# A planner that counts VectorE's maxima, reciprocals, joins and low parts of x as ready later

## Chip, core and metric

The kernel runs on one core of one Trainium2 chip. The time is device microseconds (us) from the start to the end of one execution; a kernel's figure is the median of its runs. The engines are named as in the profile: PE (TensorE, matrix products; PEld its weight loads), DVE (VectorE), ACT (ScalarE), POOL (GpSimd) and SP (SyncE, which here issues every DMA).

## What is computed

Three stages follow each other, the first per head, the other two per token:

```python
scores = q @ k.T / sqrt(D)              # 4 batches, 8 heads, 576 x 576, D = 64
kth    = the 32nd largest of each row
attn   = softmax(where(scores >= kth, scores, -1e9))
x      = attn @ v                       # 2304 tokens x 512
h      = maximum(x @ w_in, 0)           # 512 -> 2048
x      = (h * h) @ w_out                # 2048 -> 512
h      = maximum(maximum(x @ w1, x @ w2), x @ w3)   # 512 -> 768
out    = h @ w_out2                     # 768 -> 512
```

The weights come as 64-bit floats. The kernel turns each half chunk of them (128 x 1024 numbers) into a pair of 32-bit parts, high and low, and multiplies with three products (high x high, high x low, low x high). The activations x and h are split into high and low parts in the same way.

## The kernel before

The 2304 tokens are dealt into six groups of 384 columns (group 0 to group 5). For each group the attention of its rows comes first, two heads at a time (four such pairs make the 512 columns of x), then the two feed-forward stages (`moe(g)`). A piece of attention is one head by 128 rows, a *job*: PE makes scores (L525), ACT scales them into `s` (L446), DVE finds the 32 largest by four MAX (L452) with three MATCH_REPLACE between (L454), ACT makes the exponentials `e` (L312, L460, L463), POOL their low halves, SP transposes them by DMA into `et` (L468), PE multiplies with v (L479). Behind some jobs stands the end of a tile: POOL adds a guard (L530), DVE takes the reciprocal `rc` (L532), POOL multiplies (L538), PE transposes (L505), ACT writes the high part of x into `xt` (L507), DVE the low part (L509; L491 and L493 for the remainder rows).

The weights of group 0 are converted on the way, 36 half chunks during the attention of group 0 (`cw`) and 20 more during `moe(0)` (`wt`): SP loads one (L588), ACT makes two pieces of it (`ot` L312 and `lw` L592), DVE joins them by bits (L594, the *join*), ACT rounds to the high part (L597), POOL subtracts for the low part (L309), SP stores the pair in DRAM (L599). Groups 1 to 5 read the pairs back (L576).

In `moe(g)` PE makes h (L630, stage 1), ACT squares (L654 to L656), POOL makes the low part `hl`, PE makes the second product into four banks `a` (stage 2); the result is split by ACT (L667) and DVE (L668, recorded at the helper's line L309). Of the three products of the second layer ACT copies the first into `m` (L680), DVE takes the maximum with the second and the third (L682, the *maxima*), ACT and POOL split the result. The last product (the output stage) reads the weights w_out2 and goes out by ACT (L712) and SP.

No order is written by hand. Every operation is first entered in a plan, with its engine, a priority and an estimated length, and `Plan.run` plays the five engines forward on those estimates: of an engine's operations it issues the one that could begin first, a little biased by priority, and that order then stands in the program for good. An operation is ready when the last of those that it reads has ended, plus a hop between engines, plus its `slack`:

```python
        def ready_at(o):
            t = 0.0
            for d in o.deps:
                t = max(t, d.end + hop(d.eng, o.eng))
            t += o.slack
```

So slack makes no engine wait on the chip. It only makes the plan believe that the operation comes later, so that others of its engine (and, through what reads its result, of other engines) are put ahead of it. `SL` is 1000 ns. Each engine executes its own list strictly in the planned order.

Of the kernel before, what the change touches and what calls it, by code (L numbers as in the profile page):

```python
# [10 lines left out]
F32 = mybir.dt.float32  # L11
# [255 lines left out]
def kernel(ctx, tc, q, k, v, w_in, w_out, w1, w2, w3, w_out2, out):  # L267
# [34 lines left out]
    def pe(prio, ns, reads, writes, fn):  # L302
        plan.op(PE, ns, prio, reads, writes, fn)

    def dma(prio, nbytes, reads, writes, fn, ns=650.0):
        plan.op(SP, ns, prio, reads, writes, fn, lat=max(nbytes / DBW, 90.0))

    def sub(eng, out_ap, a, b):
        eng.tensor_tensor(out_ap, a, b, op=ALU.subtract)  # L309
# [108 lines left out]
    def attend(i, unit, p):  # L418
        b, tl, rem, g, col = unit
        plan.bias = -10 if i == 0 else 0  # L420
        new = (b, p) not in kv
        if new:
            kt = prep_k(b, p)
        qt = prep_q(i, unit, p)
        plan.bias = 0
        if new:
            kv[b, p] = [kt, *prep_v(load_v(b, p))]
        kt, vt, us = kv[b, p]
        if (g, p) not in xt:
            t = buf("xt", [P, 2, KD, NW], F32R)  # L430
            xt.update({(g, d): (Slot(t, 0, d), Slot(t, 1, d)) for d in range(KD)})
        xh, xl = xt[g, p]
        xg = buf("xg", [P, XW, P]) if tl else None
        xs = None
        nt = len(tl)
        jobs = [(j, h) for j in range(nt) for h in range(2)] + ([(-1, 0)] if rem else [])
        for j, h in jobs:
            for _ in range(min(PER if g == 0 else 0, len(ahead))):
                half_chunk(False, *ahead.pop(0))
            s = buf("s", [P, S])  # L440
            for f in range(2):
                ps = buf("b", [P, 512])
                cs = slice(f * HS, (f + 1) * HS)
                pe(A_S, (4 * HS / 2.4 if b in PLAIN else 2 * c_mm(HS)) * (1 if j >= 0 else 2), [kt, qt], [ps, (s, f)],
                   scores(j, h, nt, qt, kt, ps, cs, b in PLAIN))
                act(A_S, HS, [ps], [(s, f)], lambda s=s, cs=cs, ps=ps: nc.scalar.activation(  # L446
                    s[:, cs], ps[:, 0:HS], AF.Copy, scale=escale))
            w_, mx, nb, e = buf("w", [P, S]), buf("mx", [P, 32]), buf("nb", [P, 1]), buf("e", [P, S])
            for r in range(4):
                src = s if r == 0 else w_  # L450
                m8 = slice(8 * r, 8 * r + 8)
                dve(A_X, S, [src], [(mx, r)], lambda src=src, mx=mx, m8=m8: nc.vector.max(out=mx[:, m8], in_=src[:]))  # L452
                if r < 3:
                    dve(A_X, S + 50, [src, (mx, r)], [w_], lambda src=src, mx=mx, m8=m8, w_=w_: nc.vector.match_replace(  # L454
                        out=w_[:], in_to_replace=mx[:, m8], in_values=src[:], imm_value=-3.0e38))
            gps(A_E, 110, [(mx, 0), (mx, 3)], [nb], lambda mx=mx, nb=nb: nc.gpsimd.tensor_scalar(  # L456
                nb[:], mx[:, 31:32], mx[:, 0:1], ebias, op0=ALU.subtract, op1=ALU.add))
            act(A_E, S, [s, (mx, 3)], [e], lambda s=s, e=e, mx=mx: prelu(
                e[:], s[:], KEEP, bias=mx[:, 31:32], scale=-1.0), psum=False, ptr=1)
            act(A_E, S, [e, nb], [e], lambda nb=nb, e=e: nc.scalar.activation(  # L460
                e[:], e[:], AF.Exp, bias=nb[:], scale=-1.0 / KEEP), psum=False, ptr=1)
            e16, et = buf("e16", [P, 2 * S], F16), buf("et", [P, 10, P], F16)
            act(A_E, S, [e], [(e16, 0)], lambda e=e, e16=e16: nc.scalar.copy(e16[:, S:2 * S], e[:]), psum=False)  # L463
            gps(A_E, 512, [e, (e16, 0)], [(e16, 2)], lambda e=e, e16=e16: sub(
                nc.gpsimd, e16[:, 0:512], e[:, D:S], e16[:, S + D:2 * S]))
            gps(A_E, D, [e, (e16, 0)], [(e16, 3)], lambda e=e, e16=e16: sub(
                nc.gpsimd, e16[:, 512:S], e[:, 0:D], e16[:, S:S + D]))
            dma(A_S, DTR * DBW, [e16], [et], lambda e16=e16, et=et: nc.sync.dma_start_transpose(et[:, 0:9], e16[:]), ns=1360.0)  # L468
            if j < 0 or (h == 0 and j % 2 == 0):
                xs = buf("xs", [P, 2, 2, VW])  # L470
            for hh, c0, c1 in ([(0, 0, D), (1, D, P)] if j < 0 else [(h, 0, P)]):
                ps = buf("b", [P, 512])
                m = c1 - c0

                def av(ps=ps, m=m, et=et, c0=c0, c1=c1, hh=hh):
                    for x, mm_ in enumerate(AVORD):
                        wv = VW2 if mm_ < 4 else VW
                        vc = mm_ if mm_ <= 4 else mm_ - 5
                        nc.tensor.matmul(ps[0:m, 0:wv], et[:, mm_, c0:c1], vt[:, hh, vc, 0:wv],  # L479
                                         start=x == 0, stop=x == 8)  # L480
                pe(A_E, 400.0, [et, vt], [ps, (xs, (max(j, 0) % 2, hh)), *([(xg, (j, hh))] if xg else [])], av)
                act(A_X, VW, [ps], [(xs, (max(j, 0) % 2, hh))], lambda ps=ps, xs=xs, m=m, j=j, hh=hh: nc.scalar.copy(  # L482
                    xs[0:m, max(j, 0) % 2, hh, :], ps[0:m, 0:VW]))
            if j < 0:
                xr = buf("xr", [P, P])
                finish_x(xs, D, 1, xr, lambda xr=xr: xr[0:D, :].unsqueeze(1))
                ps = buf("b", [P, 512])
                pe(A_X, 107.0, [xr], [ps, (xh, "r"), (xl, "r")], lambda xr=xr, ps=ps: nc.tensor.transpose(
                    ps[:, 0:D], xr[0:D, :], ident_t[0:D, 0:D]))
                cs = slice(rcol[b], rcol[b] + D)  # L490
                act(A_X, D, [ps, us], [(xh, "r")], lambda ps=ps, cs=cs: nc.scalar.activation(  # L491
                    xh[:, cs], ps[:, 0:D], AF.Copy, scale=us[:]), ptr=1)
                dve(A_S, D, [ps, us, (xh, "r")], [(xl, "r")], lambda ps=ps, cs=cs: nc.vector.scalar_tensor_tensor(  # L493
                    xl[:, cs], ps[:, 0:D], us[:], xh[:, cs].bitcast(F32), op0=ALU.mult, op1=ALU.subtract), slack=SL / 2)
            elif h == 1 and (j % 2 == 1 or j == nt - 1):
                j0 = j - j % 2
                finish_x(xs, P, j + 1 - j0, xg, lambda j0=j0, j=j: xg[:, j0:j + 1, :])
        if not tl:
            return
        w = nt * P  # L500
        ps = buf("b", [P, 512])

        def f():
            for c in range(nt):
                nc.tensor.transpose(ps[:, c * P:(c + 1) * P], xg[:, c, :], ident)  # L505
        pe(A_S, 107.0 * nt, [xg], [ps, (xh, col), (xl, col)], f)
        act(A_S, w, [ps, us], [(xh, col)], lambda: nc.scalar.activation(  # L507
            xh[:, col:col + w], ps[:, 0:w], AF.Copy, scale=us[:]), ptr=1)
        dve(A_S, w, [ps, us, (xh, col)], [(xl, col)], lambda: nc.vector.scalar_tensor_tensor(  # L509
            xl[:, col:col + w], ps[:, 0:w], us[:], xh[:, col:col + w].bitcast(F32),  # L510
            op0=ALU.mult, op1=ALU.subtract), slack=SL / 2)

    def scores(j, h, nt, qt, kt, ps, cs, plain):
        def run():
# [13 lines left out]
    def finish_x(xs, pn, nt, dst, xo):  # L528
        rc = buf("rc", [P, 2, 2, 1])
        gps(A_S, 100, [xs], [rc], lambda: nc.gpsimd.tensor_scalar(  # L530
            rc[0:pn, 0:nt], xs[0:pn, 0:nt, :, 0:1], eguard, 2.0, op0=ALU.add, op1=ALU.mult))
        dve(A_S, 4, [rc], [rc], lambda: nc.vector.reciprocal(rc[0:pn, 0:nt], rc[0:pn, 0:nt]))  # L532

        def part(x):
            return xs[0:pn, 0:nt, :, 1 + x * D:1 + (x + 1) * D]
# [33 lines left out]
    def half_chunk(again, n, x):  # L569
# [15 lines left out]
        def word(u):  # L585
# [7 lines left out]
            lw[:], bits(U8).rearrange("p (n u) -> p n u", u=8)[:, :, 3], AF.Copy, scale=1.0 / 32.0, bias=-15.5 / 32.0), psum=False)  # L593
        joined.append(dve(C_D, 512, [cv, lw], [cv], lambda: nc.vector.scalar_tensor_tensor(  # L594
            cv[:].bitcast(U32), cv[:].bitcast(U32), 3, lw[:], op0=ALU.logical_shift_left, op1=ALU.bitwise_or),
            rate=1.7, slack=SL / 2))
        act(C_A, 512, [cv], [(wt, 0)], lambda: nc.scalar.copy(wt[:, 0], cv[:]), psum=False)  # L597
        gps(C_P, 512, [cv, (wt, 0)], [(wt, 1)], lambda: sub(nc.gpsimd, wt[:, 1], cv[:], wt[:, 0].bitcast(F32)))
        dma(W_, P * 4096, [wt], [dst], lambda: nc.sync.dma_start(  # L599
            dst[:], wt[:].rearrange("p a b -> p (a b)").bitcast(F32)))  # L600
        return wt

    def moe(g):
# [61 lines left out]
        for d in range(KD):  # L665
            xh, xl = xs[d]
            act(MA, N, [acc[d]], [(xh, kx) for kx in xcols], lambda d=d, xh=xh: nc.scalar.copy(xh[:, 0:N], acc[d][:, 0:N]))  # L667
            dve(A_S, N, [acc[d], (xh, xcols[0])], [(xl, kx) for kx in xcols], lambda d=d, xh=xh, xl=xl: sub(  # L668
                nc.vector, xl[:, 0:N], acc[d][:, 0:N], xh[:, 0:N].bitcast(F32)), slack=SL / 4)
        h2 = []  # L670
        for fp in range(NF2):
            m = [buf("m0", [P, NW]), buf("m1", [P, NW])]
            for jj in range(3):
                w_, vw = nextw()
                for f in range(2):
# [4 lines left out]
                        act(MA, N, [ps], [m[f]], lambda ps=ps, m=m[f]: nc.scalar.copy(m[:, 0:N], ps[:, 0:N]))  # L680
                    else:
                        dve(A_S, N, [ps, m[f]], [m[f]], lambda ps=ps, m=m[f]: nc.vector.tensor_tensor(  # L682
                            m[:, 0:N], ps[:, 0:N], m[:, 0:N], op=ALU.max), slack=SL / 4)
                    if jj == 2:
                        hh, hl = buf("hh", [P, NW], F32R), buf("hl", [P, NW], F32R)
                        act(MA, N, [m[f]], [hh], lambda m=m[f], hh=hh: nc.scalar.copy(hh[:, 0:N], m[:, 0:N]), psum=False)
# [104 lines left out]
```

## Time and profile before

| | us |
|---|---|
| median of 3 runs (1076.82 to 1080.04) | 1076.9 |
| the profiled execution, its own time | 1079.8 |
| its span, first to last instruction | 1078.0 |
| PE busy in the span | 984.3 |
| DVE busy | 818.7 |
| ACT busy | 767.8 |
| POOL busy | 625.3 |

The span falls into stretches with different limits. Up to 200 us the attention of group 0 runs and weights are converted; PE is busy 122 us of it. From there PE is nearly always busy, with the feed-forward of one group and the attention of later groups mixed. The groups follow each other on PE: group 1 begins at 361.8 us, group 2 at 514.6, group 3 at 670.9, group 4 at 829.4, group 5 at 955.9. From about 890 us no attention is left, and PE works on groups 4 and 5 alone.

### The profile page before, as it was taken

What the parts mean: (1) busy time and instruction counts of PE and PEld (TensorE: products, weight loads), DVE (VectorE), ACT (ScalarE), POOL (GpSimd) and SP (SyncE); (2) the same over time, 40 slices, a digit from 0 to 9 for tenths busy, and PEclk for the clock granted to TensorE, in tenths of its full rate; (3) what the DMA queues carried; (4) which work ended last, traced back from release to release, by engine and by line L of the source; (5) the groups of instructions that cost most, each with busy time, mean ns of one, the idle gap of its engine ahead of it and who ended that gap; (6) DMA issues with size and microseconds to landing.
All of it is one profiled execution on the core that took longest, in us unless ns stands there. A gap on an engine that the chain in (4) does not pass through costs nothing.

```text
span 1078.0 us, 18812 instructions
## 1 busy us (share of the span) xinstructions
PE 984.3 (91%) x6116; PEld 889.7 (83%) x6116; DVE 818.7 (76%) x1736; ACT 767.8 (71%) x1616; POOL 625.3 (58%) x887
## 2 busy tenths in 40 slices
PE   5556576999998999999999999999999999999998
PEld 3333343799897899998999998999998999989997
DVE  5999899899976999999999999999999601100020
ACT  6987788899887889976788868888876742123311
POOL 2666677787787577756467676767565641112210
PEclk9999755799999999999999999999999999999999
DMA  9999899999998999999999999999999986787774
GB/s 306 348 308 251 256 285 332 245 269 231 251 341 318 316 348 283 288 288 256 300 261 266 281 284 274 267 237 262 254 256 280 285 261 237 252 266 262 257 239 147
DMA packets 249697, 295.04 MB, mean 274 GB/s; under 512 B 178944, under 2 KB 182528, under 8 KB 249600
## 3 DMA queue, kind: packets, MB, share of 16 engines
q1 hardware_dynamic: 249600, 293.85, 95.1%
q8 instruction: 48, 0.79, 0.3%
q14 instruction: 49, 0.40, 0.1%
HBM read 217.25 MB, written 34.08 MB: 233 GB/s over the span
## 4 chain that ended last, share of the span: by engine, by line
PE 61%; DVE 13%; ACT 11%; POOL 7%; DMA 4%; issue 3%; SPq 0%; POOLq 0%; ACTq 0%; DVEq 0%
PE a L630 37%; PE b L630 13%; DVE mx L452 7%; DVE w L454 6%; PE b L525 5%; PE b L479 4%; DMA xt<-in_moe_w_in_dram 2%; POOL e L309 2%; ACT s L446 1%; ACT e L312 1%; POOL hl L309 1%; DMA xt<-in_moe_w_dram 1%; ACT lw L592 1%; ACT e L460 1%; ACT ot L312 1%
## 5 line engine op out<-in xcount | busy, mean ns | idle before, releaser
L452 DVE MAX8 mx<-w 128x8 f32<-128x576 f32 x432 | 311.1, 746 | 0.1
L309 POOL TENSOR_TENSOR e<-e,e 128x512 f16<-128x512 f32 (+1 forms) x288 | 211.9, 748 | 108.6 <-ACT e L463 91.3
L630 PE MATMUL a<-xt,wt 128*128 128x384 f32 x1296 | 239.3, 339 | 1.0 <-DVE xt L309 0.9
L630 PE MATMUL b<-xt,wt 128*128 128x384 f32 x1152 | 235.9, 346 | 3.5 <-DMA wt<-wsc 1.9
L630 PE MATMUL a<-hh,wt 128*128 128x384 f32 x768 | 228.8, 346 | 0.0
L630 PEld LDWEIGHTS a<-xt,wt 128*128 128x128 f32 x1296 | 224.1, 188 | 2.2 <-DVE xt L309 1.9
L454 DVE MATCH_REPLACE8 w<-mx,w 128x576 f32<-128x576 f32 x288 | 213.1, 742 | 0.0
L630 PEld LDWEIGHTS b<-xt,wt 128*128 128x128 f32 x1152 | 203.8, 192 | 5.8 <-DMA wt<-wsc 1.9
L525 PE MATMUL b<-kt,qt 128*128 128x288 f32 (+1 forms) x640 | 167.9, 395 | 36.2 <-DMA qt<-in_q_dram 17.8
L309 POOL TENSOR_TENSOR hl<-r,hh 128x384 fp32r<-128x384 f32 x96 | 97.3, 1014 | 126.5 <-ACT hh L656 119.2
L525 PEld LDWEIGHTS b<-kt,qt 128*128 128x128 f32 (+1 forms) x640 | 118.1, 218 | 62.5 <-ACT xs L482 16.4
L630 PEld LDWEIGHTS a<-hh,wt 128*128 128x128 f32 x768 | 142.7, 190 | 2.1 <-issue 1.1
L630 PE MATMUL a<-hl,wt 128*128 128x384 f32 x384 | 131.3, 342 | 4.1 <-POOL hl L309 3.8
L312 ACT ACTIVATE e<-s,mx 128x576 f32<-128x576 f32 x144 | 112.2, 779 | 27.7 <-POOL e L309 16.5
L479 PEld LDWEIGHTS <-et 128*128 128x128 f16 (+1 forms) x1440 | 84.1, 108 | 57.6 <-issue 35.4
L446 ACT ACTIVATE s<-b 128x288 f32<-128x288 f32 x288 | 108.0, 409 | 24.8 <-PE b L525 23.2
L479 PE MATMUL b<-vt,et 128*128 128x129 f16 (+3 forms) x1440 | 101.7, 223 | 25.2 <-DMA et<-e 16.8
L460 ACT ACTIVATE e<-e,nb 128x576 f32<-128x576 f32 x144 | 112.1, 779 | 6.8 <-POOL nb L456 4.8
L452 DVE MAX8 mx<-s 128x8 f32<-128x576 f32 x144 | 107.2, 746 | 10.3 <-ACT s L446 10.3
L454 DVE MATCH_REPLACE8 w<-mx,s 128x576 f32<-128x576 f32 x144 | 106.8, 742 | 0.0
L654 ACT ACTIVATE r<-b 128x384 f32<-128x384 f32 x96 | 47.1, 490 | 79.2 <-PE b L630 76.6
L463 ACT CAST e<-e 128x576 f16<-128x576 f32 x144 | 96.6, 672 | 1.6 <-DMA et<-e 1.3
(62 smaller groups left out, 1194.8 us busy)
## 6 DMA issues: line engine op xcount, KB each, us to landing
wt<-wsc SPq DMA_DIRECT2D x316, 512.0 KB, 4.8
wsc<-cw SPq DMA_DIRECT2D x36, 512.0 KB, 4.9
xt<-in_moe_w_out_dram SPq DMA_DIRECT2D x22, 512.0 KB, 6.3
wsc<-wt SPq DMA_DIRECT2D x20, 512.0 KB, 5.7
xt<-in_moe_w_dram SPq DMA_DIRECT2D x18, 512.0 KB, 5.9
xt<-in_moe_w_in_dram SPq DMA_DIRECT2D x16, 512.0 KB, 5.8
ks<-in_k_dram SPq DMA_DIRECT2D x12, 576.0 KB, 5.9
vst<-in_v_dram SPq DMA_DIRECT2D x16, 320.0 KB, 5.8
```

What stands on the lines that cost most here:

```text
L309: eng.tensor_tensor(out_ap, a, b, op=ALU.subtract)
L312: return nc.scalar.activation(out_ap, src, AF.Prelu, alpha=slope, **kw)
L446: act(A_S, HS, [ps], [(s, f)], lambda s=s, cs=cs, ps=ps: nc.scalar.activation(s[:, cs], ps[:, 0:HS], AF.Copy, scale=escale))
L452: dve(A_X, S, [src], [(mx, r)], lambda src=src, mx=mx, m8=m8: nc.vector.max(out=mx[:, m8], in_=src[:]))
L454: dve(A_X, S + 50, [src, (mx, r)], [w_], lambda src=src, mx=mx, m8=m8, w_=w_: nc.vector.match_replace(out=w_[:], in_to_replace=mx[:, m8], ...
L460: act(A_E, S, [e, nb], [e], lambda nb=nb, e=e: nc.scalar.activation(e[:], e[:], AF.Exp, bias=nb[:], scale=-1.0 / KEEP), psum=False, ptr=1)
L463: act(A_E, S, [e], [(e16, 0)], lambda e=e, e16=e16: nc.scalar.copy(e16[:, S:2 * S], e[:]), psum=False)
L479: nc.tensor.matmul(ps[0:m, 0:wv], et[:, mm_, c0:c1], vt[:, hh, vc, 0:wv], start=x == 0, stop=x == 8)
L525: nc.tensor.matmul(ps[:, 0:HS], a, c, start=m == 0, stop=m == len(seq) - 1)
L592: act(C_M, 512, [raw], [lw], lambda: nc.scalar.activation(lw[:], bits(U8).rearrange("p (n u) -> p n u", u=8)[:, :, 3], AF.Copy, scale=1.0 ...
L630: nc.tensor.matmul(o, x, y, start=first and i == 0 and m == 0, stop=last and i == n - 1 and m == 2)
L654: act(MA, N, [ps], [r], lambda r=r, ps=ps: nc.scalar.activation(r[:, 0:N], ps[:, 0:N], AF.Relu))
```

## The change

The slacks of five kinds of DVE operations grow: the low parts of x in the attention (L509, L493) from 500 to 1500 ns, the reciprocals (L532) from 0 to 1000, the joins (L594) from 500 to 1000, the low parts between the two feed-forward stages (L668) from 250 to 750, the maxima (L682) from 250 to 2000. DMA issues get a slack too, which is zero. No instruction is added, removed or altered; the order on all five engines is planned anew.

```diff
-            dma(A_S, DTR * DBW, [e16], [et], lambda ...: nc.sync.dma_start_transpose(et[:, 0:9], e16[:]), ns=1360.0)
+            dma(A_S, DTR * DBW, [e16], [et], lambda ...: nc.sync.dma_start_transpose(et[:, 0:9], e16[:]), ns=1360.0, slack=0.0 * SL)
...
-                    xl[:, cs], ps[:, 0:D], us[:], xh[:, cs].bitcast(F32), op0=ALU.mult, op1=ALU.subtract), slack=SL / 2)
+                    xl[:, cs], ps[:, 0:D], us[:], xh[:, cs].bitcast(F32), op0=ALU.mult, op1=ALU.subtract), slack=1.5 * SL)
...
-            op0=ALU.mult, op1=ALU.subtract), slack=SL / 2)
+            op0=ALU.mult, op1=ALU.subtract), slack=1.5 * SL)
...
-        dve(A_S, 4, [rc], [rc], lambda: nc.vector.reciprocal(rc[0:pn, 0:nt], rc[0:pn, 0:nt]))
+        dve(A_S, 4, [rc], [rc], lambda: nc.vector.reciprocal(rc[0:pn, 0:nt], rc[0:pn, 0:nt]), slack=1.0 * SL)
...
-            rate=1.7, slack=SL / 2))
+            rate=1.7, slack=1.0 * SL))
...
-                nc.vector, xl[:, 0:N], acc[d][:, 0:N], xh[:, 0:N].bitcast(F32)), slack=SL / 4)
+                nc.vector, xl[:, 0:N], acc[d][:, 0:N], xh[:, 0:N].bitcast(F32)), slack=0.75 * SL)
...
-                            m[:, 0:N], ps[:, 0:N], m[:, 0:N], op=ALU.max), slack=SL / 4)
+                            m[:, 0:N], ps[:, 0:N], m[:, 0:N], op=ALU.max), slack=2.0 * SL)
```

On DVE, near the end of group 0's attention, from the reciprocal of the fourth pair of heads (`rc3`) to its low part (`xt1`), the kernel before has:

```order
L532 RECIPROCAL rc3_1717<-rc3_1717 128x2
L454 MATCH_REPLACE w1_1672<-mx3_1656,w1_1672 128x576
L452 MAX mx2_1638<-w0_1648 128x8
L452 MAX mx3_1656<-w1_1672 128x8
L452 MAX mx4_1751<-s4_1552 128x8
L594 SCALAR_TENSOR_TENSOR ot2_1741<-ot2_1741,lw1_1674 128x512
L454 MATCH_REPLACE w1_1672<-mx3_1656,w1_1672 128x576
L509 SCALAR_TENSOR_TENSOR xt1_773<-b3_1746,us3_544,xt1_773 128x384
```

and the changed kernel, at the same place:

```order
L532 RECIPROCAL rc3_1723<-rc3_1723 128x2
L594 SCALAR_TENSOR_TENSOR ot2_1728<-ot2_1728,lw1_1657 128x512
L454 MATCH_REPLACE w1_1685<-mx3_1663,w1_1685 128x576
L452 MAX mx4_1765<-s4_1525 128x8
L452 MAX mx3_1663<-w1_1685 128x8
L454 MATCH_REPLACE w0_1777<-mx4_1765,s4_1525 128x576
L452 MAX mx5_1783<-s5_1582 128x8
L509 SCALAR_TENSOR_TENSOR xt1_759<-b2_1760,us3_591,xt1_759 128x384
```

The reciprocal and the low part have moved three places down DVE's list (247 to 250 and 254 to 257): ahead of this low part stand two MAX and one MATCH_REPLACE more than before, and the same number of joins, reciprocals and other low parts.

On PE, at the passage from group 0's second layer (weights `wt0`, `wt6`) to its output stage (w_out2 in `wt1`, `wt2`, `wt3`), the kernel before has:

```order
L630 MATMUL a1_3917<-xt1_773,wt0_3828 128x384 x6
L630 MATMUL a2_3946<-wt1_3907,hh4_3554 128x512 x2
L630 MATMUL a2_3946<-wt1_3907,hl4_3591 128x512
L630 MATMUL a3_3952<-wt1_3907,hh4_3554 128x512 x2
L630 MATMUL a3_3952<-wt1_3907,hl4_3591 128x512
L525 MATMUL b1_3963<-kt0_1439,qt0_3922 128x288 x2
L525 MATMUL b3_3967<-kt0_1439,qt0_3922 128x288 x2
L525 MATMUL b2_3970<-kt0_1439,qt0_3922 128x288 x2
```

and the changed kernel:

```order
L630 MATMUL a1_4000<-xt1_759,wt0_3849 128x384 x6
L630 MATMUL a2_4025<-wt1_3889,hh4_3627 128x512 x2
L630 MATMUL a2_4025<-wt1_3889,hl4_3652 128x512
L630 MATMUL a3_4035<-wt1_3889,hh4_3627 128x512 x2
L630 MATMUL a3_4035<-wt1_3889,hl4_3652 128x512
L630 MATMUL a0_4045<-wt1_3889,hh4_3627 128x512 x2
L630 MATMUL a0_4045<-wt1_3889,hl4_3652 128x512
L630 MATMUL a2_4025<-wt2_4056,hh5_3663 128x512 x2
```

The 24 score matmuls (twelve rows of two) that stood behind the first weights of the output stage now stand ahead of that stage, among the last products of the second layer.

On ACT, at the conversion of the weights `wt3`, the kernel before has behind the last of the twelve evictions of those scores:

```order
L446 ACTIVATE s5_4025<-b0_4031 128x288
L312 ACTIVATE ot1_4044<-xt0_143 128x512
L592 ACTIVATE lw0_4050<-xt0_143 128x512
L491 ACTIVATE xt2_2020<-b1_4035,us1_2790 128x64
L365 CAST kt0_4057<-ks0_3802 128x1152
```

and the changed kernel:

```order
L446 ACTIVATE s5_3958<-b2_3962 128x288
L365 CAST kt0_3985<-ks0_3728 128x1152
L507 ACTIVATE xt2_2115<-b1_3998,us1_3037 128x128
L312 ACTIVATE ot0_4010<-xt0_143 128x512
L592 ACTIVATE lw1_4015<-xt0_143 128x512
L312 ACTIVATE ot1_4021<-xt0_143 128x512
L592 ACTIVATE lw0_4029<-xt0_143 128x512
```

The cast of the next keys `kt0` has gone ahead of the conversions, and the pieces for `wt2` (`ot0`) now stand behind the evictions too; before, they stood ahead of them.

## Rows read from the trace of the kernel before

**Rows 1.** The page: span, then busy time, share and instructions of an engine.

```profile
span 1078.0 us, 18812 instructions
PE 984.3 (91%) x6116; PEld 889.7 (83%) x6116; DVE 818.7 (76%) x1736; ACT 767.8 (71%) x1616; POOL 625.3 (58%) x887
```

**Rows 2.** Stretches: length, busy us of PE, PEld, DVE, ACT, POOL, clock, DMA, GB/s.

```profile
0.00:200.00 200.00, 122.34 (x437) 76.57 (x438) 178.89 (x362) 165.59 (x332) 126.20 (x164) 0.81 0.99 296
200.00:290.00 90.00, 90.00 (x641) 82.78 (x640) 82.72 (x190) 78.79 (x177) 68.24 (x111) 0.97 0.97 246
290.00:361.00 71.00, 65.24 (x384) 58.60 (x383) 54.57 (x102) 59.45 (x123) 56.91 (x60) 0.95 0.97 323
361.00:515.00 154.00, 150.51 (x1027) 142.72 (x1028) 151.86 (x329) 126.20 (x269) 101.82 (x146) 1.00 1.06 296
515.00:671.00 156.00, 154.74 (x1082) 146.77 (x1082) 154.47 (x334) 124.61 (x267) 106.05 (x158) 1.00 1.03 273
671.00:829.00 158.00, 157.92 (x1128) 147.77 (x1127) 152.97 (x339) 127.95 (x283) 102.19 (x169) 1.00 1.02 259
829.00:1078.00 249.00, 243.59 (x1425) 234.46 (x1423) 43.21 (x88) 85.20 (x170) 63.89 (x80) 1.00 0.77 248
```

**Rows 3.** Waits of DVE from 0 to 200: us in total, times, longest us.

```profile
DVE ot L594 <- ACT ot L312: 4.3, 7, 0.9
...
DVE ot L594 <- ACT lw L592: 2.4, 1, 2.4
DVE rc L532 <- POOL rc L530: 1.4, 2, 0.8
DVE xt L509 <- ACT xt L507: 0.5, 1, 0.5
```

**Rows 4.** Chain of waits, start and us: three MAX, two MATCH_REPLACE end to end.

```profile
134.81 1.98 DVE mx L452 x3
136.79 1.46 DVE w L454 x2
```

**Rows 5.** Groups by line, DVE, 0 to 201.6: busy us, mean ns, idle before.

```profile
L594 DVE SCALAR_TENSOR_TENSOR ot<-ot,lw 128x512 uint32<-128x512 uint32 x39 | 32.8, 840 | 6.9 <-ACT ot L312 4.3 <-ACT lw L592 2.4
```

**Rows 6.** Timeline, DVE and POOL near 88: start, us; two joins, one POOL subtraction.

```profile
88.08 1.18 DVE L594 SCALAR_TENSOR_TENSOR ot<-ot,lw 128x512 uint32<-128x512 uint32 x1 [0.39 <-ACT ot L312]
...
91.17 0.67 DVE L594 SCALAR_TENSOR_TENSOR ot<-ot,lw 128x512 uint32<-128x512 uint32 x1
...
87.55 1.15 POOL L309 TENSOR_TENSOR e<-e,e 128x512 f16<-128x512 f32 x1 [1.03 <-ACT e L463]
```

**Rows 7.** Timeline near 188: group 0's last low part; PE before and at its use.

```profile
187.03 0.61 DVE L509 SCALAR_TENSOR_TENSOR xt<-b,us,xt 128x384 fp32r<-128x384 f32 x1
...
186.01 4.20 PE L525 MATMUL b<-kt,qt 64*128 64x288 f32 x8
...
190.91 1.31 PE L630 MATMUL b<-xt,wt 128*128 128x384 f32 x3
```

**Rows 8.** Timeline from 338 to 350: PE in the output stage, ACT, POOL.

```profile
346.85 0.79 PE L630 MATMUL a<-wt,hh 128*128 128x512 f32 x1 [1.25 <-ACT wt L597]
349.33 0.79 PE L630 MATMUL a<-wt,hh 128*128 128x512 f32 x1 [1.69 <-POOL wt L309]
...
338.95 3.15 ACT L446 ACTIVATE s<-b 128x288 f32<-128x288 f32 x10
...
344.57 3.03 POOL L309 TENSOR_TENSOR kt<-ks,kt 64x1152 fp32r<-64x1152 f32 x1 [3.32 <-ACT kt L365]
```

**Rows 9.** Timeline near 510: group 2's last low part, PE's first use of it.

```profile
506.77 0.61 DVE L509 SCALAR_TENSOR_TENSOR xt<-b,us,xt 128x384 fp32r<-128x384 f32 x1
...
514.64 0.69 PE L630 MATMUL b<-xt,wt 128*128 128x384 f32 x3
```

**Rows 10.** DVE's waits for the maxima, from 361 to 829, then 829 to 1078.

```profile
DVE m L682 <- PE a L630: 2.6, 7, 0.5
...
DVE m L682 <- PE a L630: 60.9, 24, 5.8
```

More of the change, by code (lines that the diff above doesn't have):

```diff
@@ L303, in pe, with dma @@
         plan.op(PE, ns, prio, reads, writes, fn)
-    def dma(prio, nbytes, reads, writes, fn, ns=650.0):
-        plan.op(SP, ns, prio, reads, writes, fn, lat=max(nbytes / DBW, 90.0))
+    def dma(prio, nbytes, reads, writes, fn, ns=650.0, slack=0.0):
+        plan.op(SP, ns, prio, reads, writes, fn, lat=max(nbytes / DBW, 90.0), slack=slack)
     def sub(eng, out_ap, a, b):
@@ L467, in attend @@
                 nc.gpsimd, e16[:, 512:S], e[:, 0:D], e16[:, S:S + D]))
-            dma(A_S, DTR * DBW, [e16], [et], lambda e16=e16, et=et: nc.sync.dma_start_transpose(et[:, 0:9], e16[:]), ns=1360.0)
+            dma(A_S, DTR * DBW, [e16], [et], lambda e16=e16, et=et: nc.sync.dma_start_transpose(et[:, 0:9], e16[:]), ns=1360.0, slack=0.0 * SL)
             if j < 0 or (h == 0 and j % 2 == 0):
@@ L599, in half_chunk @@
         dma(W_, P * 4096, [wt], [dst], lambda: nc.sync.dma_start(
-            dst[:], wt[:].rearrange("p a b -> p (a b)").bitcast(F32)))
+            dst[:], wt[:].rearrange("p a b -> p (a b)").bitcast(F32)), slack=0.0 * SL)
         return wt
```

## The prediction

> **What bounds the kernel now.** I read the page's first lines, then the busy times by stretch, then DVE's waits, and last the timelines at three places. The page puts PE first, busy 984.3 of 1078.0 us, DVE second with 818.7 [rows 1]. The stretches say more [rows 2]. Up to 200 us PE is busy 122.3 us and DVE 178.9: here DVE, with ACT at 165.6 beside it, decides when group 0's x is complete, and PE has little else to do. From 200 to 290 PE has no idle time. From 290 to 361 it is idle 71.0 - 65.2 = 5.8 us. From 361 to 829 it is idle 3.5 + 1.3 + 0.1 = 4.9 us in 468, and DVE is as full (151.9, 154.5 and 153.0 us of 154, 156 and 158). From 829 on PE works alone, with 243.6 of 249 us busy, the empty end of the span included, and DVE at 43.2. PE's total of work does not change. So the end moves only by what PE idles before 361 us, and by what would become idle later.
>
> **The change, part by part.** Nothing is added or removed; each part is a shift in the lists.
>
> *Start, 0 to 200 us.* DVE's waits on the kinds that move are 4.3 us for joins waiting for ACT's piece `ot` (seven, the longest 0.9), 2.4 for one join waiting for `lw`, 1.4 for two reciprocals, 0.5 for one low part [rows 3]. A step of DVE costs 1.98 / 3 = 0.66 us for a MAX and 1.46 / 2 = 0.73 for a MATCH_REPLACE end to end [rows 4]. Half a microsecond more of slack lets at least one such step go ahead of a join, which covers a wait of the mean size, 4.3 / 7 = 0.61, and leaves some 0.2 of the longest: I count 4.0 of 4.3 as gone. The reciprocals' 1.4 and the low part's 0.5 are shorter than their new slack: gone. The one of 2.4 lies at the very start, where DVE has little to put ahead: stays. Together 5.9 us less. Against it, two MAX and one MATCH_REPLACE more stand ahead of the fourth low part, 2 x 0.66 + 0.73 = 2.05 us. So that low part can end 3.8 us earlier; between 3.8 earlier (all of this) and 2.1 later (no wait goes). But PE did not stand waiting for it: it ended at 187.64, and PE, with eight score matmuls from 186.01 on ahead, used it at 190.91 [rows 7], 3.3 us later. Those matmuls depend on ACT's evictions and on free banks, which only partly follow DVE. I take half: **-1.9 us**, between -3.8 and +2.1.
>
> *Output stage of group 0, 290 to 361 us.* PE idles 5.8 us [rows 2]. 1.25 and 1.69 of it are one wait for the weights `wt3`, behind ACT's rounding and then POOL's subtraction; ahead of them ACT evicted ten score pieces (3.15 us), and POOL stood with the subtraction for the next keys (3.03 us) in front [rows 8]. The changed order puts the 24 score matmuls, their evictions and the cast of those keys earlier. PE's work ahead of `wt3` is the same, but ACT and POOL are free of these two pieces sooner. That favours `wt3`. `wt2` loses: before, its pieces were made ahead of the evictions, now behind. So a part of the wait returns one weight tile earlier. I take back the wait ended by POOL, 1.7, and half of the one ended by ACT, 0.6: **-2.3 us**, between -5.8 (all idle time goes) and +2.0 (the 2.94 us of both waits stay and two thirds as much is added at `wt2`).
>
> *Rule against trace.* PE's weight loads are busy 82.5% of the stretch 290 to 361, 93.4% of 361 to 829 and 94.2% of the tail [rows 2]. The Trainium skill, page "Perfetto Trace Analysis", section "Identifying the Most-Contended Engine", says that TensorE's headroom is to be judged by the share of its weight loads and not by that of its matmuls. By that rule the stretch 290 to 361 holds (94.2 - 82.5)% x 71 = 8.3 us and not 5.8, so the sum could be 2.5 us lower at most; I keep to the idle time.
>
> *Low parts of later groups.* Ahead of group 2's last low part stand three MAX and three MATCH_REPLACE more, 3 x 1.39 = 4.2 us. It ended at 507.4 and PE used it at 514.64 [rows 9]: 7.3 us of cover. If PE comes 4.2 us earlier, 3.1 are left, but DVE comes earlier too, by the waits that go. **0 us**, at worst +1 (4.2 + 4.2 - 7.3 = 1.1). This is also what is late next: no more than about 7 us can be gained ahead of group 2 without DVE itself gaining.
>
> *Maxima.* From 361 to 829 DVE waits 2.6 us for them in all [rows 10], and PE is nearly never idle there: 0. In the tail DVE waits 60.9 us because it has nothing else to do; PE's list from the start of group 4's stage 1 is the same in kind, and what is queued behind a later maximum (ACT's cast of h, and now ACT's next copy ahead of it) feeds the output stage only. **0 us**, within +-0.5.
>
> *Low parts between the feed-forward stages, DMA issues.* The first stand close together on DVE in both orders, with one or two short steps among them; the DMA slack is zero, and the DMA order moves only with the rest. **0 us**, within +-0.5.
>
> The sum is -1.9 - 2.3 = -4.2 us. The profiled execution took 1079.8 us, 1.8 more than its span, and is 2.9 above the median; the change should act alike on both, so I set it against the median: 1076.9 - 4.2 = **1072.7 us**.
>
> **The rivals.**
>
> *The waits only change their owner.* ACT is busy 165.6 us of the first 200 [rows 2], and a join that no longer waits for `ot` only shows that DVE did something else; if ACT's own list sets the end of group 0, DVE's saved time becomes idle time elsewhere, and in the output stage `wt2` takes over `wt3`'s wait. Then 0 to -2 us: 1076. For it: PE used the fourth low part 3.3 us after it was there [rows 7]. Against it: DVE is the fuller of the two.
>
> *The joins run into POOL: slower.* A join alone takes 0.67 us; the one at 88.08 took 1.18, and ended 0.56 after the POOL subtraction that ran from 87.55 to 88.70 [rows 6]. So a join that starts under a POOL operation stands until that ends, and its DVE list with it. The 39 joins up to 201.6 us have a mean of 0.84 [rows 5], so 39 x 0.17 = 6.6 us are spent this way already; where each join meets POOL is left to chance by a new order. If the mean rose to 1.18, DVE would lose 39 x 0.34 = 13.3 us against the 3.8 gained, less 3.3 of cover at PE: 13.3 - 3.8 - 3.3 = +6.2, 1083. The gain is used up from a mean of 0.84 + 3.8 / 39 = 0.94 on. For it: the mean of 0.84 says that a part of them meet POOL already; against it: that nearly all should is unlikely, since POOL is busy 126 of 200 us in any order. The Trainium skill, page "SBUF — State Buffer", section "SBUF: two separate sides", states the same as a rule: a VectorE operation with two SBUF inputs and a GpSimd operation that reads SBUF lock each other out for a whole instruction. The rows agree with it.
>
> *All of it goes.* The fourth low part's 3.8 us and PE's 5.8 us of idle time between 290 and 361: -9.6, 1067.3. For it: PE has nothing else to do at either place; against it: the join of `wt2` has got further back.
>
> **How the numbers follow.** The forecast (1070 to 1073.6) has 0.31, the waits that change owner (1073.7 to 1080.1) 0.32, the joins against POOL 0.23, all of it 0.14. The first two are nearly level; the forecast stands with "all of it goes" on one side, so the predicted time is taken there, 1072.7. About 0.3% (3.2 us) is what a measurement of this kernel can tell from no change. Faster by more: 0.31 + 0.14 = 0.45; within: 0.32; slower: 0.23. For the range I add the ends: -3.8 - 5.8 = -9.6, and -1.7 if the joins meet POOL less (a quarter of 6.6): 1065.6; above, +2.1 + 2.0 + 1.1 = +5.2: 1082.1, just below the price of the joins' rival, which leaves out its upper half and little of the lower end.
>
> **What would show it.** In the profile after: DVE's waits for joins, reciprocals and low parts up to 200 us, 8.6 us now, should be near 3; the fourth low part should end near 184, and PE's use of it be near 189; PE's idle time from 290 to 361 should be near 3.5 us, with the wait at `wt2` or `wt3`; group 1 should start near 357.5 on PE, group 2 near 510.5 with no wait for a low part, and the tail from group 4's start should be as long as now (1078.0 - 829.4 = 248.6). It is wrong if the joins' mean up to 200 us is over 0.94, if PE waits for group 2's low parts, or if the time comes from stretches after 361 us, where I see nothing to win.

## The result and the profile after

The changed kernel takes 1087.34 us (median of 4 executions, 1086.39 to 1088.12), the one before 1076.86 measured beside it. The ratio is 1.0087, with a 95% interval from 1.0062 to 1.0111. So it is 0.9% slower where I forecast 0.4% faster, and outside the range. Its profiled execution took 1087.95 us, with a span of 1086.2: 8.2 us more than the span of before. (The medians lie 10.5 apart, mostly since the profiled execution of before was 2.9 us above its median.) The rows answer to [rows 1] and [rows 2] (columns as there):

```profile
span 1086.2 us, 18805 instructions
PE 988.5 (91%) x6116; PEld 891.2 (82%) x6116; DVE 819.7 (75%) x1736; ACT 768.4 (71%) x1616; POOL 624.0 (57%) x887
```

```profile
0.00:200.00 200.00, 121.09 (x436) 77.04 (x436) 176.99 (x358) 164.63 (x328) 125.09 (x162) 1.00 1.00 296
200.00:290.00 90.00, 88.51 (x613) 80.41 (x613) 82.86 (x190) 77.56 (x175) 66.61 (x109) 0.93 0.91 232
290.00:361.00 71.00, 65.11 (x395) 59.52 (x394) 53.41 (x96) 58.15 (x122) 53.38 (x60) 0.96 0.98 319
...
829.00:1086.00 257.00, 250.70 (x1470) 240.10 (x1467) 46.82 (x96) 90.60 (x184) 66.21 (x85) 1.00 0.79 247
```

DVE has the same work and is not fuller. PE is busy 4.2 us longer in all, with as many matmuls, and waits more. The clock of 1.00 up to 200 us is no gain: the clock records of this trace begin at 195.4 us, and a stretch without records reads as full. Four score matmuls at 188.41 take 2.28 us, the pace of the half clock (eight take 4.21 below), and in a second trace of the same kernel (e9 below) the records show half from 121.4 to 193.1.

```profile
188.41 2.28 PE L525 MATMUL b<-kt,qt 64*128 64x288 f32 x4
```

Where the loss begins is seen from one mark on PE's list in both traces: the first matmul of group 0's second layer (`a<-xt`), behind the last of its stage 2. First before, then after:

```profile
292.33 0.79 PE L630 MATMUL a<-xt,wt 128*128 128x384 f32 x3
```

```profile
298.20 1.13 PE L630 MATMUL a<-xt,wt 128*128 128x384 f32 x5
```

It comes 5.9 us later. Of the whole 8.2 us of span 5.9 are there at 298 us, ahead of the output stage. (Rounded, the whole is made of +1.1 up to the first low part, +1.0 from there to the fourth, +3.8 to the mark, -1.3 to group 3's start and +3.5 from there to the end.) The fourth low part, on which my first step rests [rows 7], and DVE's waits up to 200 us, beside [rows 3]:

```profile
189.13 0.62 DVE L509 SCALAR_TENSOR_TENSOR xt<-b,us,xt 128x384 fp32r<-128x384 f32 x1 [0.61 <-ACT xt L507]
```

```profile
DVE us L383 <- ACT sc L381: 5.3, 4, 3.6
DVE ot L594 <- ACT ot L312: 4.9, 6, 2.2
DVE ot L594 <- ACT lw L592: 1.8, 1, 1.8
DVE xt L509 <- ACT xt L507: 0.6, 1, 0.6
DVE rc L532 <- POOL rc L530: 0.3, 1, 0.3
```

The joins still wait 4.9 us where 4.3 stood; only the reciprocals' wait went. The low part ends 2.1 us later (187.6 to 189.7), the mark 5.9 later: 3.8 us are lost between the two. There TensorE's granted clock differs. Stretches of before, then of after (PEclk is the last column but two; 0.50 is the 1.2 GHz level, 1.00 the 2.4 GHz level):

```profile
197.00:200.00 3.00, 1.92 (x6) 1.09 (x6) 1.77 (x6) 3.00 (x8) 3.00 (x5) 0.85 1.01 354
200.00:203.00 3.00, 3.00 (x9) 2.24 (x9) 3.00 (x7) 1.80 (x5) 2.83 (x6) 0.50 1.01 375
203.00:206.00 3.00, 3.00 (x20) 2.56 (x19) 2.65 (x6) 0.77 (x2) 0.24 (x1) 0.51 1.22 245
206.00:209.00 3.00, 3.00 (x21) 2.54 (x20) 0.82 (x4) 2.92 (x7) 2.24 (x6) 1.00 1.05 148
```

```profile
197.00:200.00 3.00, 2.66 (x8) 1.55 (x8) 2.50 (x4) 2.97 (x6) 3.00 (x5) 0.80 1.00 385
200.00:203.00 3.00, 1.51 (x3) 0.50 (x2) 3.00 (x8) 2.87 (x7) 3.00 (x5) 0.50 0.78 272
...
206.00:209.00 3.00, 3.00 (x8) 1.89 (x6) 3.00 (x7) 1.45 (x3) 1.42 (x2) 0.50 0.93 252
209.00:212.00 3.00, 3.00 (x9) 2.62 (x9) 3.00 (x6) 1.92 (x3) 1.50 (x2) 0.50 0.17 21
212.00:215.00 3.00, 3.00 (x29) 2.54 (x29) 1.94 (x6) 1.65 (x5) 2.49 (x2) 0.92 1.02 268
```

The trace's clock events put the return to full at 205.9 us before and at 212.5 after. It is a second return: the clock had been at full already, from 195.7 to 199.1 us before and from 195.4 (where the records begin) to 198.8 after, and fell once more. PE's timeline in these stretches, before and then after, shows what it did around that: `a<-hh` and `a<-hl` are stage 2's first twelve matmuls, L525 are scores, two matmuls each. (The expectations of e13 to e16 call stage 2 the second layer, and the mark its end; those of e9 to e11 call the mark the start of the second layer.)

```profile
196.62 0.44 PE L630 MATMUL a<-hh,wt 128*128 128x384 f32 x1
...
197.96 0.75 PE L525 MATMUL b<-kt,qt 64*128 64x288 f32 x2 [0.23 <-ACT xs L482]
199.51 1.32 PE L525 MATMUL b<-kt,qt 64*128 64x288 f32 x2 [0.80 <-ACT s L446]
...
208.07 2.20 PE L525 MATMUL b<-kt,qt 64*128 64x288 f32 x8
```

```profile
197.34 0.45 PE L630 MATMUL a<-hl,wt 128*128 128x384 f32 x1 [0.90 <-POOL hl L309]
...
201.77 1.32 PE L525 MATMUL b<-kt,qt 64*128 64x288 f32 x2 [1.49 <-ACT s L446]
...
205.24 4.21 PE L525 MATMUL b<-kt,qt 64*128 64x288 f32 x8
```

Eight score matmuls take 2.20 us at the full clock and 4.21 at the half one. In PE's list before, the twelve stand as three, two scores, nine; after the change as three, four scores, six, four scores, three. The scores have to wait for ACT to empty their banks, and the rest of the twelve stands behind them.

### The profile page after: what moved, and what is told of

Same layout as the page of the kernel before. It is cut to its first block, busy times and chain, and to the rows that moved or that the text cites. A ratio compares the mean times of both kernels' runs of the same rounds, so it can differ in the third digit from the quotient of the medians.

```text
span 1086.2 us, 18805 instructions
## 1 busy us (share of the span) xinstructions
PE 988.5 (91%) x6116; PEld 891.2 (82%) x6116; DVE 819.7 (75%) x1736; ACT 768.4 (71%) x1616; POOL 624.0 (57%) x887
## 5 line engine op out<-in xcount | busy, mean ns | idle before, releaser
L525 PE MATMUL b<-kt,qt 128*128 128x288 f32 (+1 forms) x640 | 169.3, 400 | 33.3 <-DMA qt<-in_q_dram 18.4
L525 PEld LDWEIGHTS b<-kt,qt 128*128 128x128 f32 (+1 forms) x640 | 120.0, 221 | 59.4 <-ACT s L446 13.2
L479 PE MATMUL b<-vt,et 128*128 128x129 f16 (+3 forms) x1440 | 100.6, 222 | 31.3 <-DMA et<-e 18.8
L654 ACT ACTIVATE r<-b 128x384 f32<-128x384 f32 x96 | 47.2, 491 | 79.4 <-PE b L630 78.8
```

The lines of the kernel that those rows point to most:

```text
L525: nc.tensor.matmul(ps[:, 0:HS], a, c, start=m == 0, stop=m == len(seq) - 1)
L654: act(MA, N, [ps], [r], lambda r=r, ps=ps: nc.scalar.activation(r[:, 0:N], ps[:, 0:N], AF.Relu))
```

## The experiments

Ratios are against the kernel before, measured beside each group (1078.5 to 1078.9 us), with 95% intervals. From each trace I read five pieces, each from times rounded to 0.1 us: from the first low part to the fourth, from the fourth to the clock's last return to full ahead of the mark, from the fourth to the mark, from the mark to group 3's start on PE, and from there to the end of PE's last matmul (3.6 us ahead of the span's end in every trace).

```
kernel                ratio   low1-4  clock   mark  mark-g3  g3-end
before                        106.8   18.3   104.7   378.6   403.5
changed               1.0087  107.8   22.8   108.5   377.3   407.0
e9  changed again     1.0069  107.3   23.5   108.4   377.9   407.0
e1  maxima            1.0049  107.1   16.9   104.2   381.1   403.5
e2  reciprocals       0.9981  110.1    8.4    99.1   378.5   403.0
e3  low parts         1.0045  107.7    9.4   102.0   382.9   403.7
e4  joins             1.0041  113.9    8.7    99.8   383.0   404.0
e5  joins 490 ns      1.0015  107.2   17.6   104.5   376.0   406.4
e6  maxima 0          1.0027  106.8   17.3   104.2   380.5   401.9
e10 first only        1.0023  108.7   16.5   105.4   373.8   406.8
e11 later only        1.0000  107.3   18.4   104.6   379.2   403.1
e12 gaps filled       1.0048  107.3   22.5   107.9   380.0   407.0
e13 without low       1.0082  111.4   24.7   110.1   377.2   403.3
e14 without rc        1.0040  112.0   10.3   100.6   379.2   405.5
e15 scores behind     1.0039  107.5   11.0   103.0   377.6   407.0
e16 before, behind    0.9976  106.8    8.0   100.8   378.9   403.5
```

**One part alone.** Four kernels, each with one of the new slacks (in e1 also that of the low parts between the feed-forward stages; of the edits the telling lines are shown).

```diff
 e1: +m[:, 0:N], ps[:, 0:N], m[:, 0:N], op=ALU.max), slack=2.0 * SL)
 e2: +nc.vector.reciprocal(...), slack=1.0 * SL)
 e3: +op0=ALU.mult, op1=ALU.subtract), slack=1.5 * SL)
 e4: +rate=1.7, slack=1.0 * SL))
```

> The kernel before with the larger slacks on the maxima (2000 ns) and on the low parts between the feed-forward stages (750 ns) alone. The lists are the same as before up to about 290 us. Theory A (the loss of the change is made before 215 us, where TensorE comes back to full clock 6.6 us later): no more than +3 us, 1077 to 1080, with the first third of the span as before. Theory B (the later maxima hold banks of PSUM and cost PE time in every second layer): +4 to +8 us, 1081 to 1085.

> The kernel before with the larger slack on the reciprocals alone. Theory A1 (later planned reciprocals and low parts put off the end of group 0's attention, each by its share): +2 to +4 us, and full clock back some 2 to 4 us after 206. Theory A2 (any new order of the first 200 us moves the moment at which PE comes to full clock, whichever operation was meant): anything from -6 to +8 us, with the time going with that moment and not with the slack.

> The kernel before with the larger slack on the low parts of x in the attention alone. Theory A1 (the low parts come later by their slack): +2 to +4 us, and the fourth low part ends at 189 to 190 instead of 187.6. Theory A2 (the moment of full clock is moved by any new order): anything from -6 to +8 us, and the time goes with that moment.

> The kernel before with the larger slack on the joins alone. Theory A1: 0 to -3 us, since the joins' waits of 6.7 us up to 200 shorten and no low part is put off. Theory A2 (any new order moves the moment of full clock): anything from -6 to +8 us, and the time goes with that moment.

Measured: 1.0049 [1.0030, 1.0067], 0.9981 [0.9961, 1.0000], 1.0045 [1.0028, 1.0062] and 1.0041 [1.0029, 1.0054]. None of the four loses anything from the fourth low part to the mark, where the changed kernel loses most. e1, e3 and e4 lose 2.5, 4.3 and 4.4 us from the mark to group 3 instead, where the changed kernel loses nothing; in e3 PE waits there 4.4 us for ACT's `wt` and 3.1 for POOL's, where 1.2 and 1.7 stood. e2 shows no loss.

**Is slack as such dear?** A hardly changed slack for the joins, and none for the maxima and the low parts between the feed-forward stages.

```diff
 e5: -rate=1.7, slack=SL / 2))
     +rate=1.7, slack=SL * 0.49))
 e6: -op=ALU.max), slack=SL / 4)
     +op=ALU.max), slack=0.0)
```

> The kernel before with the joins' slack at 490 instead of 500 ns: 10 ns, fifty times less than the change makes it, and the other way. It still gives another order: 735 of DVE's 1306 places differ from the kernel before, from place 209 on (some 155 us). Theory L (any new order of this plan costs or gives a few us, whatever the slack means): 1 to 6 us off the kernel before, to either side. Theory S (a larger slack costs because operations come later by it): within 1.5 us of the kernel before.

> The kernel before with no slack on the maxima and on the low parts between the feed-forward stages (250 ns before, 2000 and 750 in the change). Theory S (the later the plan believes the maxima, the longer banks are held): -0.5 to -1.5 us, a seventh of what the larger slack cost, with the other sign. Theory L (a new order is a new draw): 1 to 6 us off, to either side.

Measured: 1.0015 [0.9997, 1.0034] and 1.0027 [1.0009, 1.0045]. More slack for the maxima and less are both slower, so the price is not in the size of the slack: here theory S fell. e5 alone, 0.9 us above the kernel before, tells nothing: it is within S's 1.5 us and just short of L's 1. But its pieces moved by -2.6 us from the mark to group 3 and by +2.9 behind that. A new order from the mark on moves that part by up to 5 us either way (373.8 to 383.0 in the table).

**Zeros between TensorE's work.**

```diff
+            if id(o) in fill:    # every operation of PE ahead of stage 2
+                self.warm(3)     # three 128x512 matmuls of zeros
```

> The kernel before, in its own order, with three matmuls of zeros (128x512, two-byte) into a bank that is free then, behind each of PE's 112 operations ahead of the first product of group 0's second stage: 336 in all, which no result reads. Theory C (PE at half clock up to 206 us costs time, in the scores and in the first products of group 0): full clock much earlier, the first low parts earlier, -3 to -8 us. Rival: DVE sets the pace up to 190 us and the zeros only stand in PE's way: +1 to +5 us.

> The changed kernel with the same zeros. Theory C: it gains at least 3 us more than the kernel before does by them, since its full clock came 6.6 us later, and ends within 7 us of the kernel before with zeros. Rival (the 10 us come from the order alone): it stays 9 to 11 us above the kernel before with zeros.

Measured: 1.0385 [1.0310, 1.0461] and 1.0498 [1.0441, 1.0555]. The zeros stood in the way of the real work, far beyond the rival's 5 us too, and told nothing of the clock. My theory in this form fell. e8 stays 8.0 us above e7, between what the theory (within 7) and its rival (9 to 11) gave.

**The changed kernel again, its two halves in time, and its two waits filled.** e10 has the new slacks only on what is built ahead of group 0's feed-forward, e11 only on the rest; e12 puts five zero matmuls at PE's two waits near 197 and 201 us.

```diff
 e10: +slack=(1.5 if plan.first else 0.5) * SL    # e11 the other way round; joins, reciprocals alike
 e12: +fill = {id(pes[stop - 1]): 2, id(pes[stop + 3]): 3}    # stop: first op of stage 2
```

> The changed kernel once more, beside the three below. Theory T (the loss at the start is a property of the order): TensorE's granted clock goes back to full at 212 to 213 us again, the second layer of group 0 starts at 297 to 299 us (before: 292.3), and the ratio lies between 1.007 and 1.011. Rival N (the moment of full clock is chance, another one in each run): the clock is back by 206 us and the second layer starts near 295, with a ratio nearer 1.005.

> The changed slacks only for operations made ahead of group 0's feed-forward (its low parts, its reciprocals, its joins); all others keep the slack of before. VectorE's list is that of the changed kernel up to its row 256 (the fourth low part), then it departs. Theory T (about 6 of the 10 us are lost at the start): second layer of group 0 at 296 to 299 us, ratio 1.004 to 1.007. Rival R (the loss belongs to the later groups, and the start's lateness is regained): 1.000 to 1.002, with the end within 2 us of before.

> The other half: the changed slacks only for operations made from group 0's feed-forward on. VectorE's list is that of before up to its row 269 (about 200 us). Theory T: second layer of group 0 at 291 to 293 us as before, full clock at 204 to 206 us, and 3 to 5 us lost later on: ratio 1.003 to 1.005. Rival R: 1.007 to 1.010, the whole loss.

> The changed kernel with five matmuls of zeros on TensorE (128x512, into a bank that is not in use yet; no result reads them): two behind the matmul that ends at 195.8 us, ahead of the wait for POOL's hl (0.90 us shown), three ahead of the score matmul that waits 1.49 us for ACT's s at 201.8. VectorE's list is that of the changed kernel. Theory C (TensorE's two waits at 196 to 202 us are why its clock returns 6.6 us later than before): with the waits filled the granted clock is full from 204 to 207 us, eight score matmuls at 205 us take 2.2 and not 4.2 us, the second layer starts 2 to 3.5 us earlier than in the changed kernel of the same session, and the ratio falls by 0.002 to 0.003. Rival D (the clock's return has another cause, or the zeros delay the real matmuls as in the fill before): full from 212 us as before or later, ratio the same or up to 0.002 higher.

Measured: 1.0069 [1.0046, 1.0093], 1.0023 [1.0008, 1.0037], 1.0000 [0.9982, 1.0017] and 1.0048 [1.0028, 1.0068]. By absolute times e9 missed theory T (clock at 210.2 and mark at 295.2, not 212 to 213 and 297 to 299). It shows what belongs to the order: its first low part ends 2.6 us earlier than in the other execution (79.4 against 82.0), but from there on both agree within 0.7 us in each piece. The halves don't add up to the whole, and both ratios lie below those that theory T gave (1.004 to 1.007 and 1.003 to 1.005): e10's list departs from the changed one at the fourth low part, and its clock returns 6.3 us sooner. In e12 the waits were not filled; rows of its trace:

```profile
198.02 0.82 PE L339 MATMUL a<-wsrc 128*128 128x512 bf16 x3
200.25 1.11 PE L540 MATMUL b<-kt,qt 64*128 64x288 f32 x2 [1.40 <-ACT s L461]
...
203.50 4.21 PE L540 MATMUL b<-kt,qt 64*128 64x288 f32 x8
```

The zeros ran in 0.82 us, and PE still waited 1.40 us behind them. The clock fell a little later (200.5 us, where 198.8 stood) and came back at 210.7, 22.5 us behind the fourth low part as before. The lower ratio fits theory C's number, the clock does not, so it says nothing for C.

**The order at stage 2.** The table shows a pattern: where the twelve matmuls stand in a row (e2, e3, e4), the clock is back 8 to 9 us behind the fourth low part; where eight scores cut them, 23. e10 does not fit it as it stands: there the twelve are in a row too, but behind four scores and a wait, and the clock is back after 16.5 us. Rows of its PE:

```profile
200.83 1.33 PE L526 MATMUL b<-kt,qt 64*128 64x288 f32 x2 [2.13 <-ACT s L447]
202.09 0.69 PE L631 MATMUL a<-hh,wt 128*128 128x384 f32 x1
```

Counted from the first of the twelve instead, e10 fits as well (206.3 - 202.1 = 4.2 us). Of the kernels with one part left out, the changed kernel without the low parts' slack (e13) keeps the eight scores, without that of the reciprocals (e14) it has the twelve in a row.

> The changed kernel, but with the attention's low parts at their old slack. Where the second layer of group 0 begins, TensorE's list reads as in the changed kernel: three second-layer matmuls, four scores, six second-layer, four scores, three second-layer (before: three, two scores, nine). Theory O (these scores in the row put off the return of TensorE's clock): full clock 22 to 24 us behind the end of the fourth low part (before 18.3, changed 22.8), from that low part to the end of the second layer (start of the next stage's matmuls) 107.5 to 109 us (before 104.7, changed 108.5), ratio 1.005 to 1.009. Rival Q (the late low parts cost it): full clock 17 to 19 us behind, 104 to 105 us, ratio at most 1.002.

> The changed kernel, but with the reciprocals at their old slack. TensorE's list where the second layer of group 0 begins is now two scores, twelve second-layer matmuls in a row, two scores. Theory O: full clock 8 to 11 us behind the end of the fourth low part (as in the kernels with one part alone that read so: 8.4, 9.4 and 8.7), then 99 to 102 us to the end of the second layer; the time is lower than the changed kernel's by 3 us or more, ratio 1.000 to 1.005. Rival Q: the low parts stay late, so ratio 1.006 to 1.009 and 108 us.

Measured: 1.0082 [1.0064, 1.0100] and 1.0040 [1.0025, 1.0055], clock and mark as in the table: O held, Q fell (e13's 24.7 and 110.1 lie a little above O's ranges, on the side away from Q). Here the parts interact: reciprocals and joins together give the bad row, neither alone does. (e13 has the maxima's slack too, but e1 with that alone has the row of before.)

**Only the scores moved.** The decisive pair: the other three accumulators' first operations go directly behind the first one's, in TensorE's list alone.

```diff
+        acc = [o for o in seq if o.eng == PE and any(b.tag == "a" for b in o.opens)][:4]
+        seq = [o for o in seq if o not in acc[1:]]
+        n = seq.index(acc[0]) + 1
+        seq[n:n] = acc[1:]
```

> The changed kernel with nine matmuls moved on TensorE alone: the second layer's first twelve stand in a row, and the eight scores that cut them follow behind. All other engines' lists are the changed kernel's. Theory O: full clock 8 to 14 us behind the end of the fourth low part, 100 to 105 us to the end of the second layer, ratio 0.003 to 0.007 under that of the changed kernel in its two measurements (1.0087 and 1.0069). Rival M (the clock returns after a certain amount of work whatever its order): 22 to 24 us, 108 us, same ratio as the changed kernel; later scores could even cost 1 to 2 us between 300 and 361 us.

> The kernel before with the same move: two scores go behind the second layer's first twelve matmuls. Theory O: full clock 8 to 14 us behind the end of the fourth low part and not 18.3, 2 to 5 us less to the end of the second layer, ratio 0.995 to 0.999. Rival M: 17 to 19 us, 104 to 105 us, ratio 0.9985 to 1.0015.

Measured: 1.0039 [1.0023, 1.0055] and 0.9976 [0.9961, 0.9991], with the clock back after 11.0 and 8.0 us: O held in both, M fell. The interval of e15 lies below that of the changed kernel's first measurement (1.0062 to 1.0111) and overlaps that of its second (1.0046 to 1.0093). e16, at 1076.79 us against 1078.58, beats both kernels, by 0.24% the one before. Rows of e15 (its score run, the mark), then of e16 (stretches, scores, the mark):

```profile
198.95 4.32 PE L530 MATMUL b<-kt,qt 64*128 64x288 f32 x16
...
290.68 0.79 PE L635 MATMUL a<-xt,wt 128*128 128x384 f32 x3
```

```profile
194.00:197.00 3.00, 2.88 (x11) 1.71 (x10) 2.37 (x5) 3.00 (x9) 3.00 (x3) 0.87 0.80 247
197.00:200.00 3.00, 3.00 (x15) 2.25 (x14) 2.39 (x7) 2.98 (x8) 3.00 (x4) 1.00 0.98 362
200.00:203.00 3.00, 3.00 (x30) 2.50 (x28) 3.00 (x6) 1.68 (x5) 2.42 (x7) 1.00 1.02 376
```

```profile
195.74 0.44 PE L635 MATMUL a<-hh,wt 128*128 128x384 f32 x1
...
198.44 1.23 PE L530 MATMUL b<-kt,qt 64*128 64x288 f32 x4
...
203.04 2.20 PE L530 MATMUL b<-kt,qt 64*128 64x288 f32 x8
...
287.63 0.62 PE L635 MATMUL a<-xt,wt 128*128 128x384 f32 x2
```

From the fourth low part to the mark e15 needs 5.4 us less than the changed kernel (103.0 against 108.4 in e9), e16 3.9 less than the kernel before (100.8 against 104.7); every other piece is what it was within 0.3. Two things went together. One is the wait: from the first of the twelve to the eight score matmuls e16 takes 203.04 - 195.74 = 7.30 us where before took 208.07 - 196.62 = 11.45; of these 4.15 us 1.03 are the waits of 0.23 and 0.80 that are gone. The other 3.1 fit the clock, which is at full from 194.8 to 341.5 us in e16, and was at half for 6.8 us of this piece before: half pace on 6.8 us costs 3.4 at most.

Over all kernels, counted from the first of the twelve, the clock is back for good within 5.2 us where they stand in a row (e2, e3, e4, e10, e14, e15; in e16 it is back 1.0 us ahead of them), after 8.5 to 9.3 us where two scores cut them (before, e1, e5, e6, e11), and after 16.3 to 18.8 where eight do (changed, e9, e12, e13). What keeps it down in between stays open: in e13 PE is busy 14.9 of the 15 us from 200 to 215, nearly without waits, and the clock stays at half to 215.2; in e15 sixteen score matmuls in a row run at the full clock, and it stays full. The Trainium skill, page "TensorE: Matmul & The Clock Gate", section "Loop structure matters more than you think", says that the loop nest determines whether the matmuls stay at the full clock, and gives as the bad case a wait for a DMA in front of every matmul. e15 and e16 agree as far as the order goes: it alone brings the full clock 11.8 and 10.3 us earlier, though PE waits for ACT and POOL in these rows and for no DMA.

## Why the prediction was wrong

- **Start, -1.9: this step failed.** I let a shift of the fourth low part pass to PE by half and priced nothing between it and the end of group 0. In e2 to e4 that low part is 2.6 to 3.1 us later than before, and the mark comes no later (289.6 to 292.2 against 292.3). In the changed kernel the low part is 2.1 us later and the mark 5.9. What was missing is a term for PE's own order at stage 2, which measured 3.8 us: scores between its matmuls that wait for a bank, and the clock behind them. [Rows 2] showed the clock at 0.81 up to 200 us and 0.97 from 200 to 290; I gave it no price.
- **DVE's waits, 5.9 of 8.6 to go: wrong.** 7.6 us stay (4.9 + 1.8 + 0.6 + 0.3; up to the fourth low part alone 5.4 of 7.4), the waits for `us` grew from 3.1 to 5.3, and the longest join wait is 2.2 us. The low part's own part of the loss is small: 0.5 to 1.0 us from the first low part to the fourth (e9 and the first trace), against my 2.05; the other 1.1 of the 2.1 us lie ahead of the first low part, where two executions of the changed kernel differ by 2.6.
- **Output stage, -2.3: wrong; the rival was right here.** PE idles 71.0 - 65.11 = 5.9 us, as before. The wait for ACT's `wt` fell from 1.2 to 0.3, but scores now wait 1.9 for ACT and `xr` 1.0 for POOL; from the mark to group 1 are 69.2 us, before 69.5. Waits of PE from 290 to 361:

```profile
PE b L525 <- ACT s L446: 1.9, 1, 1.9
PE a L630 <- POOL wt L309: 1.6, 1, 1.6
PE b L488 <- POOL xr L538: 1.0, 1, 1.0
...
PE a L630 <- ACT wt L597: 0.3, 1, 0.3
```

- **Later low parts, 0: right.** Group 2's ends at 516.0, PE uses it at 520.2; the cover shrank from 7.3 to 4.2 us and held.
- **Maxima, 0 within 0.5: mis-sized alone, right in the whole.** e1 loses 2.5 us from the mark to group 3; e11, with the maxima among its slacks, loses 0.6 there and nothing in its ratio (1.0000).
- **The tail "as long as now": wrong by 1.7.** From group 4's start on it takes 1086.2 - 835.9 = 250.3 us, not 248.6. PE's waits for `hl` from 829 to 1078 (before: 1.7 in three) read now:

```profile
PE a L630 <- POOL hl L309: 2.5, 4, 0.6
PE a L630 <- ACT hh L656: 0.3, 2, 0.2
```

  With what group 3 takes longer (160.4 against 158.5), this is the 3.5 us that e15 does not give back. e11 has the new slacks there and not this loss, e10 has it without them: it is once more an order and no price of slack. Why this one costs it stays open.
- **The rival of joins against POOL: fell,** though its time (1083) was the nearest. 39 joins up to 203 us, beside [rows 5], with a mean of 838 ns where 840 stood:

```profile
L594 DVE SCALAR_TENSOR_TENSOR ot<-ot,lw 128x512 uint32<-128x512 uint32 x39 | 32.7, 838 | 7.1 <-ACT ot L312 4.9 <-ACT lw L592 1.8
```

## What to carry to other kernels

Where a planner sets the order, a slack on one engine is a new order on all of them, and its effect is not the sum of its parts: read the new list of the engine that bounds each stage, at the places where its work begins anew, before counting what waits less elsewhere. On PE, look there for matmuls that wait for a bank to be emptied and stand between ones that need no bank emptied, and move these few by hand; in the kernel before that gained 0.24% with an interval clear of 1, which no change of slack did.

## What the hardware showed that I had not expected

The return of TensorE's clock, between 8 and 25 us behind the same low part, goes with nearly all of the spread in the length of the stretch up to the mark: in the four traces where it returned after 22.5 to 24.7 us (mean 23.4) the mark came after 108.7 us on average, in the six with 8.0 to 11.0 (mean 9.3) after 100.9, which is 0.55 us for each us; the other six lie between (16.5 to 18.4, and 104.2 to 105.4). Half pace alone would give 0.5 at most, and the two pairs that differ in this order alone give 0.47 and 0.38 (5.5 us for 11.8 in e15, 3.9 for 10.3 in e16). That the waits that go with it are the rest is not shown. Nine matmuls moved in one list change the return by 12 us. And two executions of one program differ by 2.6 us up to the first low part, at 80 us, and by 0.7 at most in each piece behind it: here the scatter between executions arose at the start.
